# Where the output projection's weights are loaded, and a re-cut order, in a fused attention and MLP kernel

## The chip, the cores and the metric

The kernel runs on one core of a Trainium2 chip. The metric is the device time of one execution in microseconds; the time before is the median of three runs. The profile is of one further execution.

## What is computed

```
xn  = layernorm(x)                                   # 2048 tokens x 640
q   = (xn @ wq) as 32 heads of 20;  k = xn @ wk;  v = xn @ wv   # one k and v for all heads
A   = softmax(q k^T / sqrt(20)) v, heads joined, @ wo
B   = silu(xn @ w1) @ w2                             # 640 -> 1728 -> 640
out = x + A + B
```

All inputs and the output are bf16.

## The kernel before

A scheduler written in Python lays out the whole program before it is built. Each step is an `Op` with an engine, an estimated duration and the steps that it depends on; the scheduler gives every engine a fixed list, in which it runs on the chip, with semaphores where one engine needs another's result.

The work is cut into four chunks of 512 queries (`QC`, `QW`), and each chunk into 8 groups of 4 heads, 32 groups in all. A group has 64 score blocks: 4 heads by 16 tiles of 128 keys. TensorE makes each block (line 1090, one head in one of the four row groups of the array, so that up to four run side by side) into one of 7 PSUM banks of 512 columns. A block is then turned into softmax weights by one of two engines. ScalarE takes one, two or three neighbouring banks at a time by an exponential (line 1114). Or VectorE clamps one block to integers (line 1130); three such make a set, and two shifted copies of it are added up by VectorE (1594) or GpSimd (1600). TensorE multiplies the weights with v in steps of up to four matmuls, one for each head, in four column groups (line 1168), into an eighth bank. At the end of a group VectorE casts that bank to SBUF (`Uev`, line 1644, tensor sbt13), SP issues a DMA transpose of it (line 1613, into sbt14), VectorE takes the reciprocal of the sums (line 1627), and GpSimd scales (1632).

Between these, TensorE works off jobs (line 649): the projection of q for the next chunk, the MLP's two layers and the output projection for the last one. A job is done in whole steps of four column groups, or a step is cut into four quarter pieces that ride in a run of scores (line 1268). VectorE evicts q (line 1745, tensor sbt5), and SP then copies it head by head to its place in sbt9 (line 1754, five to eight DMAs for each).

From the 64th score block on TensorE's list isn't planned but written out by hand: `ORDER` has one letter for each step (a or A a score block for ScalarE, where A closes the exponential; d or D one for VectorE; p a step of PV; j a whole step of a job; k a quarter piece), `BANKS` the bank of each, and `SETS` which blocks each p takes. The other engines' lists follow from it by the scheduler's rules. On SP, DMAs of the names `dma` and `xTd` go in the order in which they were made; the others go when the scheduler finds them ready. An `Op` with a time in `at` isn't placed ahead of that time of the plan (lines 345 to 346); `RES_AT` is 96.0, and the eight residual loads (`load_res`, line 1931) have it.

The tensor qT (sbt9) has two halves, for the chunk in work and for the next. Before q may be copied in, a half is filled from `qo` (sbt19) by one DMA (`qz`, line 2244; 1 MB for the half of chunk 1). `late_loads` is called at the end of group 0 (`norm_dma`, line 1610, when `g == LATE_G`) and makes the loads that can't go sooner, since the first stage uses that memory: 15 loads of w2 (sbt3, line 2033), 5 of wo (sbt6, line 2254) and the fill. After the fill VectorE zeroes a part of `qo` (line 2257).

## Time and profile before

| | |
|---|---|
| runs | 676.49, 677.92, 678.03 us; median 677.92 |
| profiled execution | 676.2 us, of which 674.4 us are the span from first to last instruction |
| PE, ACT busy | 99%, 97% of the span |
| DVE, POOL busy | 93%, 82% |
| DMA, mean busy share of 16 engines | 0.17 |
| exponentials of line 1114 | 680, busy 597.7 us |
| loads of wo | 5 of 160 KB, issued by SP from 60.64 us on |

Line numbers are those of the kernel before. PE is TensorE's matmuls, PEld its weight loads, DVE VectorE, ACT ScalarE, POOL GpSimd, SP the queue that issues nearly all DMAs. Times in the timelines count from the start of the span. A timeline's row is merged from neighbours of one line: start, duration, engine, line, operation, output and input, count, and in brackets the idle time ahead with what ended it.

### The profile page before, as it was taken

The numbers are of one execution on the slowest core, as the hardware profiler recorded it, in microseconds if no ns is written. First come the engines' busy times: TensorE is split into PE (matmuls) and PEld (weight loads), VectorE is DVE, ScalarE is ACT, GpSimd is POOL, SyncE is SP. The second block draws the span as 40 slices with busy tenths as digits, with TensorE's granted clock in tenths as the row PEclk, the third lists the DMA queues.
The fourth block names the chain that finished last, engine by engine and source line by source line (L and its number), as shares of the span: only waits on it lengthen the run. The fifth ranks groups of instructions, "written<-read, shape, count | busy, mean of one in ns | idle before, by whom it ended". The sixth has DMA issues, their size and how long they took to land.

```text
span 674.4 us, 22180 instructions
## 1 busy us (share of the span) xinstructions
PE 666.3 (99%) x9683; PEld 224.6 (33%) x9686; DVE 629.7 (93%) x1130; ACT 653.5 (97%) x790; POOL 556.1 (82%) x440
## 2 busy tenths in 40 slices
PE   9999999999999999999999999999999999999998
PEld 4333233323332333333333333333333333233344
DVE  7998899999999999999999999999999999999994
ACT  6999899999999999999999999999999999999994
POOL 5577798788877898888889889988888889988892
PEclk9999899999999999999999999999999999999999
DMA  7557130001013000020103001101012010000012
GB/s 208 106 187 236 49 93 10 10 18 10 18 23 51 10 11 9 18 37 18 29 18 69 22 10 10 26 16 31 10 29 66 20 29 10 8 4 20 20 27 75
DMA packets 53239, 28.14 MB, mean 42 GB/s; under 512 B 39094, under 2 KB 52502, under 8 KB 53142
## 3 DMA queue, kind: packets, MB, share of 16 engines
q1 hardware_dynamic: 52854, 26.40, 15.5%
q8 instruction: 76, 1.25, 0.7%
q10 hardware_dynamic: 288, 0.33, 0.2%
q14 instruction: 21, 0.17, 0.1%
HBM read 11.44 MB, written 2.62 MB: 21 GB/s over the span
## 4 chain that ended last, share of the span: by engine, by line
PE 93%; DVE 4%; ACT 1%; POOL 1%; DMA 0%; issue 0%; ACTq 0%
PE psall L1168 33%; PE psall L1090 28%; PE psall L649 27%; DVE sbt L1130 2%; PE psall L1353 1%; ACT sbt L1549 1%; POOL sbt L1600 1%; PE psall L1526 1%; PE psall L1441 1%; PE psall L1268 1%; PE psall L2285 1%; PE psall L1775 0%; DMA sbt<-sbt 0%; DVE sbt L1594 0%; DVE sbt L1566 0%
## 5 line engine op out<-in xcount | busy, mean ns | idle before, releaser
L1114 ACT ACTIVATE sbt<-psall 128x1024 bf16<-128x1024 f32 (+1 forms) x680 | 597.7, 1036 | 5.2 <-PE psall L1090 4.6
L1600 POOL TENSOR_TENSOR sbt<-sbt 128x768 int32<-128x768 int32 (+1 forms) x369 | 520.6, 1437 | 91.2 <-DVE sbt L1594 83.0
L1130 DVE TENSOR_SCALAR sbt<-psall 128x512 int16<-128x512 f32 x703 | 452.9, 682 | 24.8 <-PE psall L1090 15.7
L1168 PE MATMUL psall<-sbt 128*32 128x512 bf16 x3410 | 280.4, 385 | 0.0
L1090 PE MATMUL psall<-sbt 32*128 32x512 bf16 x1967 | 251.5, 385 | 1.7 <-DVE sbt L1130 1.3
L649 PE MATMUL psall<-sbt 128*32 128x320 bf16 (+1 forms) x3663 | 228.7, 332 | 0.0
L1090 PEld LDWEIGHTS psall<-sbt 32*128 32x128 bf16 x1967 | 66.7, 91 | 229.4 <-ACT sbt L1114 89.2
L649 PEld LDWEIGHTS psall<-sbt 128*32 128x32 bf16 x3663 | 80.5, 95 | 83.6 <-issue 47.9
L1168 PEld LDWEIGHTS psall<-sbt 128*32 128x32 bf16 x3410 | 68.8, 95 | 100.6 <-issue 76.8
L1594 DVE TENSOR_SCALAR sbt<-sbt 128x1536 int16<-128x1536 int16 (+1 forms) x129 | 72.9, 581 | 0.3
L1268 PE MATMUL psall<-sbt 32*128 32x320 bf16 (+1 forms) x200 | 64.7, 325 | 0.2 <-DVE sbt L1130 0.2
L1794 DVE SCALAR_TENSOR_TENSOR sbt<-sbt,psall 128x512 bf16<-128x512 bf16 (+1 forms) x56 | 37.9, 679 | 0.7 <-ACT sbt L1786 0.4
L1786 ACT ACTIVATE sbt<-psall 128x512 bf16<-128x512 f32 x54 | 38.2, 708 | 0.0
L1549 ACT ACTIVATE sbt<-psall 128x1024 bf16<-128x1024 f32 (+2 forms) x28 | 27.8, 1071 | 0.3 <-PE psall L1526 0.2
L1632 POOL TENSOR_TENSOR sbt<-sbt 128x320 bf16<-128x320 bf16 x31 | 22.5, 727 | 3.5 <-DVE sbt L1594 2.7
L1644 DVE CAST sbt<-psall 128x512 bf16<-128x512 f32 x31 | 21.1, 681 | 0.0
L1268 PEld LDWEIGHTS psall<-sbt 32*128 32x128 bf16 x200 | 18.0, 90 | 5.5 <-issue 2.4
L1892 DVE SCALAR_TENSOR_TENSOR sbt<-psall,sbt 128x320 bf16<-128x320 f32 x28 | 13.3, 486 | 5.4 <-PE psall L649 3.9
L1353 PE MATMUL psall<-sbt 128*128 128x512 bf16 (+4 forms) x57 | 15.7, 422 | 1.4 <-DVE sbt L2048 1.2
L2140 POOL TENSOR_SCALAR sbt<-sbt 128x640 bf16<-128x640 bf16 x9 | 7.8, 874 | 10.6 <-DVE sbt L2144 10.5
L1566 DVE TENSOR_SCALAR sbt<-psall 128x512 int16<-128x512 f32 x22 | 14.8, 686 | 1.0 <-PE psall L1526 0.8
L2114 DVE BATCH_NORM_STATS2 sbt<-sbt 128x6 f32<-128x320 bf16 x26 | 11.4, 472 | 2.5 <-DMA sbt<-in_A_x_dram 2.5
(84 smaller groups left out, 125.6 us busy)
## 6 DMA issues: line engine op xcount, KB each, us to landing
sbt<-in_A_x_dram SPq DMA_DIRECT2D x31, 160.0 KB, 3.0
out_dram<-sbt SPq DMA_DIRECT2D x15, 160.0 KB, 1.8
sbt<-in_B_w_dram SPq DMA_DIRECT2D x5, 432.0 KB, 6.1
sbt<-sbt SPq DMA_DIRECT2D x105, 20.0 KB
sbt<-in_B_w_dram SPq DMA_DIRECT2D x13, 160.0 KB, 3.0
sbt<-sbt SPq DMA_DIRECT2D x1, 1024.0 KB, 5.8
sbt<-sbt SPq DMA_TRANSPOSE x58, 2.5
sbt<-in_A_wo_dram SPq DMA_DIRECT2D x5, 160.0 KB, 3.3
```

What stands on the lines that cost most here:

```text
L649: ins = pe.matmul(self.bk(b, 0, n, j, j + SLOT), w[:, j:j + SLOT], x, start=start, stop=stop, tile_position=(0, j), skip_group_check=True)
L1090: return pe.matmul(self.bk(b), self.kT[row:row + SLOT, kt * P:(kt + 1) * P], self.qT[row:row + SLOT, g % 8, (g // 8) % 2, :], start=True, ...
L1114: return a.activation(self.E[:, b0 * QW:(b0 + n) * QW], self.ps[:, b1 * BANK:(b1 + n) * BANK], AF.Exp, scale=ACT_SCALE, bias=ACT_BIAS)
L1130: return v.tensor_scalar(self.Z[:, zs, zp * QW:(zp + 1) * QW], self.bk(b), 0.0, ZMAX, ALU.max, ALU.min)
L1168: ins = pe.matmul(self.bk(UBANK, 0, QW, r, r + SLOT), self.v[:, it.w, it.kt, :], it.x(), start=f, stop=False, tile_position=(0, r), skip_g ...
L1268: return pe.matmul(self.bk(b, 0, n), w[r0:r0 + SLOT, :], x[r0:r0 + SLOT, :], start=first, stop=last, tile_position=(r0, 0), skip_group_che ...
L1549: return a.activation(self.E[:, (b0 + lo) * QW:(b0 + lo + m) * QW], self.ps[:, b * BANK:(b + m) * BANK], AF.Exp, scale=ACT_SCALE, bias=ACT ...
L1594: sc.new("dve", td, lambda v, k=k: v.tensor_scalar(self.Y[:, zs, k, 0:w], self.Z[:, zs, 0:w], float(PH[k + 1][0]), None, ALU.add), zk, yk, ...
L1600: sc.new("pool", tp, lambda v, k=k, cb=cb: v.tensor_tensor(self.Y[:, zs, k, 0:w].bitcast(I32), self.Z[:, zs, 0:w].bitcast(I32), cb, ALU.ad ...
L1632: op = sc.new(eng, 0.75 if eng == "pool" else t_dve_ps(16 * DH), lambda v: v.tensor_tensor(dst, ut[:, :, :, 0:DH], rb, ALU.mult), [key, (" ...
L1786: sc.new("act", t_act(QW), lambda a: a.activation(t, src, AF.Tanh, scale=0.5), [("B", b)], [("tb", tp)], prio=X_PRIO, name=f"th{c}_{fk}")
L1794: sc.new("dve", t_dve_ps(QW), lambda v, r0=r0, r1=r1, ht=ht: v.scalar_tensor_tensor(out=ht[r0:r1, :], in0=t[r0:r1, :], scalar=1.0, in1=src ...
```

## The change

In `late_loads` the fill is made ahead of wo's loads, and wo's loads get `RES_AT` as their earliest time. The tables `ORDER`, `BANKS` and `SETS` are replaced as a whole; the shares of their letters stay nearly the same (3925 letters become 3915).

```
@@ load_w
                 op.deps = set(deps)
                 op.inc_no = len(pieces)
+                if key == "o":
+                    op.at = RES_AT
             sc.note(op, (), [tag])
@@ late_loads
             load_w2([key])
+            qz(1, [key])
             load_w("sp", "o", [lambda q, c=c: q.dma_start(self.wo[:, c, :], self.A_wo[c * P:(c + 1) * P, :])
                                for c in range(DC)], ("wo",), P * D * 2, (), [key])
-            qz(1, [key])
@@ ORDER
-    "ppaADppdaAaAddppDApaDaApppAAkpjdaAkjjjaAdkppdakAppaAkjpppDDaApjjaADkppDaAkjpaDkAjjjjjdaAppaADppDaAdp"
...
+    "paADpppDaAaAddpppdAApppaDAapDApjjDaAjjaAjppaADpaAkjpjpDaAdjpjaAdkppaAdkpkadApjjjjjadAppaAdppdaAppDa"
...
```

The first place is SP's list from group 0's transposes (the first row, sbt14 from sbt13) to group 1's (the last). The difference of the two programs, with - for before and + for the change; the line numbers behind the edit go up by two or three.

```order
 L1613 DMA_TRANSPOSE sbt14<-sbt13 128x4x128
-L2033 DMA sbt3<-in_B_w2_dram 128x640 x13
-L2033 DMA sbt3<-in_B_w2_dram 64x640 x2
-L2254 DMA sbt6<-in_A_wo_dram 128x640 x5
-L2244 DMA sbt9<-sbt19 128x8x512
+L2035 DMA sbt3<-in_B_w2_dram 128x640 x13
+L2035 DMA sbt3<-in_B_w2_dram 64x640 x2
+L2246 DMA sbt9<-sbt19 128x8x512
 L1754 DMA sbt9<-sbt5 12x512
 L1754 DMA sbt9<-sbt5 20x512 x5
 L1754 DMA sbt9<-sbt5 16x512
 L1613 DMA_TRANSPOSE sbt14<-sbt13 128x4x128
```

The five loads of wo have left; the fill follows w2 directly, and the rest stands as it stood. In the batch of copies behind the last row one copy of 4 rows moves from the sixth place to the first.

The second place is SP's list where wo's loads have gone, from the residual loads (sbt21 and sbt20) to the transposes of group 3.

```order
 L1931 DMA sbt21<-in_A_x_dram 128x640 x4
 L1931 DMA sbt20<-in_A_x_dram 128x640 x4
+L2257 DMA sbt6<-in_A_wo_dram 128x640 x5
 L1613 DMA_TRANSPOSE sbt14<-sbt13 128x4x128
 L1754 DMA sbt9<-sbt5 20x512 x6
```

They stand behind all eight residual loads and ahead of these transposes.

The third place is VectorE's list in the changed program, from the cast of group 1's sums (L1644) over their reciprocal (L1627) to the zeroing of `qo`, which is L2259 here. L1130 evicts scores, L1794 is the MLP's, and L1745 evicts q.

```order
L1644 CAST sbt13<-psall 128x512
L1130 TENSOR_SCALAR sbt11<-psall 128x512 x3
L1794 SCALAR_TENSOR_TENSOR sbt15<-sbt18,psall 128x512
L1130 TENSOR_SCALAR sbt11<-psall 128x512
L1745 TENSOR_SCALAR sbt5<-psall 128x512
L1130 TENSOR_SCALAR sbt11<-psall 128x512
L1627 RECIPROCAL sbt31<-sbt14 128x16
L1130 TENSOR_SCALAR sbt11<-psall 128x512 x7
L2259 MEMSET sbt19 64x256
```

The list of before has the same rows from the cast to the reciprocal; behind it four evictions stood ahead of the zeroing, where seven stand now.

## The prediction

> **What bounds the kernel now.** First the page's first part, for the engines' shares.

> ```profile
> PE 666.3 (99%) x9683; PEld 224.6 (33%) x9686; DVE 629.7 (93%) x1130; ACT 653.5 (97%) x790; POOL 556.1 (82%) x440
> ```

> Two engines are full, TensorE and ScalarE. Which waits for which is asked of the table of waits (engine, line and what it waited for; us in total, times, longest):

> ```profile
> PEld psall L1090 <- ACT sbt L1114: 89.2, 239, 0.6
> ...
> ACT sbt L1114 <- PE psall L1090: 4.6, 4, 2.8
> ...
> DVE sbt L1627 <- DMA sbt<-sbt: 2.1, 2, 1.9
> ```

> Score matmuls (L1090) wait 239 times for an exponential (L1114) to empty a bank; the exponentials wait for scores only 4 times, and one of those waits is 2.8 of the 4.6 us. So ScalarE paces the middle of the kernel, and anything that lets ScalarE run dry is added to the time. The third row is a rare thing beside it: VectorE's reciprocal of a group's sums (L1627) waited for a DMA, once for 1.9 us. To see whether the two belong together I cut the time into windows (busy us and count of PE, PEld, DVE, ACT, POOL; then granted clock, DMA share, GB/s).

> ```profile
> 66.00:68.00 2.00, 2.00 (x36) 0.66 (x24) 2.00 (x5) 2.00 (x3) 2.00 (x3) 1.00 1.08 385
> 68.00:70.00 2.00, 2.00 (x30) 0.62 (x26) 1.98 (x4) 2.00 (x4) 2.00 (x2) 1.00 0.43 138
> 70.00:72.00 2.00, 2.00 (x33) 0.48 (x25) 1.69 (x3) 2.00 (x3) 2.00 (x3) 1.00 0.11 32
> 72.00:74.00 2.00, 1.06 (x14) 0.31 (x10) 0.46 (x2) 2.00 (x5) 1.28 (x2) 1.00 0.33 76
> 74.00:76.00 2.00, 1.60 (x13) 0.55 (x17) 2.00 (x4) 0.58 (x2) 2.00 (x3) 0.58 0.08 21
> 76.00:78.00 2.00, 2.00 (x19) 0.32 (x11) 0.95 (x3) 0.59 (x1) 1.45 (x2) 0.56 0.09 23
> ```
> ```profile
> PEclk9999899999999999999999999999999999999999
> ```

> They do. VectorE is nearly idle from 72 to 74 us, then TensorE, then ScalarE (0.58 and 0.59 of 2 us), and from 74 to 78 us the granted clock is 0.58 and 0.56. The page's slices of the clock, each 16.9 us, show no other dip: the one 8 holds this place.

> VectorE's timeline (start, duration, line; in brackets the idle time before it) shows who was late:

> ```profile
> 60.37 0.68 DVE L1745 TENSOR_SCALAR sbt<-psall 128x512 bf16<-128x512 f32 x1
> ...
> 66.71 0.68 DVE L1644 CAST sbt<-psall 128x512 bf16<-128x512 f32 x1
> ...
> 71.01 0.68 DVE L1130 TENSOR_SCALAR sbt<-psall 128x512 int16<-128x512 f32 x1
> 73.54 0.25 DVE L1627 RECIPROCAL sbt<-sbt 128x16 f32<-128x16 bf16 x1 [1.85 <-DMA sbt<-sbt]
> ```

> Group 1's sums are cast to SBUF at 66.71 to 67.39 us, and the reciprocal that needs them transposed is reached at 71.69. That is 4.3 us, and it was not enough. The SP queue's timeline and a row of the chain of waits tell why.

> ```profile
> 53.06 7.54 SPq L2033 DMA_DIRECT2D sbt<-in_B_w_dram  x15
> 60.64 3.25 SPq L2254 DMA_DIRECT2D sbt<-in_A_wo_dram  x5
> 63.94 0.70 SPq L2244 DMA_DIRECT2D sbt<-sbt  x1
> 64.76 5.81 SPq L1754 DMA_DIRECT2D sbt<-sbt  x7
> 71.02 1.25 SPq L1613 DMA_TRANSPOSE sbt<-sbt  x1
> ...
> 94.65 3.90 SPq L1931 DMA_DIRECT2D sbt<-in_A_x_dram  x8
> 112.78 1.21 SPq L1613 DMA_TRANSPOSE sbt<-sbt  x1
> ```
> ```profile
> 71.02 2.50 DMA sbt<-sbt
> ```

> The transposes (L1613) stand behind 15 loads of w2, 5 of wo, the fill of q's other half (L2244) and 7 copies of q. SP was busy from 53.06 to 70.57 without a gap worth naming, so they went out at 71.02, though their data stood ready at 67.39, and landed 2.50 later, at 73.52.

> **The change, part by part.** *The five loads of wo leave the place ahead of the fill.* Their row is 3.25 us of SP, 3.29 to the start of the fill. The fill then starts at 60.64 and the seven copies at 64.76 - 3.29 = 61.47. The first copy also waits for VectorE's L1745, which ended at 61.05, so that doesn't hold it. Seven copies take 5.81 and end at 67.28; the cast ends at 67.39, so the transposes go out at about 67.5 and land at 70.0. VectorE reaches the reciprocal at 71.69: 1.7 us to spare instead of 1.85 short. The order of VectorE between cast and reciprocal is the same in both programs (third piece of order above), so nothing moves this meeting point but the work ahead. The data in the DMA engines doesn't stand against it: their share was 1.08 at 66 to 68 us and 0.43 after, with wo's 0.8 MB (5 x 128 x 640 x 2 bytes) among it; without it the backlog ends sooner. Behind the transposes SP's next batch of copies now begins with the 4-row copy, which waits for the seven copies; issued by 67.28, they have the transposes' own 2.50 us and more to land, so it holds nothing. What is late next is nothing on VectorE's queue: the steps behind the reciprocal are evictions of scores that were waiting.

> What is the wait worth? TensorE and ScalarE around it:

> ```profile
> 71.41 0.61 PE L1168 MATMUL psall<-sbt 128*32 128x512 bf16 x8
> 71.96 0.39 PE L1090 MATMUL psall<-sbt 32*128 32x512 bf16 x3
> 72.28 0.40 PE L1168 MATMUL psall<-sbt 128*32 128x512 bf16 x4
> 72.61 0.45 PE L1090 MATMUL psall<-sbt 32*128 32x512 bf16 x3
> 74.40 0.60 PE L1090 MATMUL psall<-sbt 32*128 32x512 bf16 x1 [1.33 <-DVE sbt L1130]
> 74.93 1.90 PE L1168 MATMUL psall<-sbt 128*32 128x512 bf16 x16
> 76.76 0.61 PE L1090 MATMUL psall<-sbt 32*128 32x512 bf16 x4
> 77.30 0.59 PE L1168 MATMUL psall<-sbt 128*32 128x512 bf16 x4
> 77.83 0.39 PE L1090 MATMUL psall<-sbt 32*128 32x512 bf16 x3
> ```
> ```profile
> 77.41 2.96 ACT L1114 ACTIVATE sbt<-psall 128x1024 bf16<-128x1024 f32 x4 [2.83 <-PE psall L1090]
> ```

> By ScalarE it is 2.83 us, its idle time. By TensorE: starts at full clock are 0.32 us after a run of scores, 0.33 after one step of four PV matmuls, and 0.22 more for each further step (0.55 for two). From 72.61 stand a run of four scores, four PV steps, a run and one step: 0.33 + 0.99 + 0.32 + 0.33 = 1.97, so 77.83 should have been 74.58, and the loss is 3.25. The engine that sets the pace is ScalarE, so I take **-2.83** and keep -3.25 for the range. The 1.33 us of idle is less than half of either; the rest is the clock.

> [...]

> *The loads of wo come back behind the eight residual loads*, at about 98.6 us (94.65 + 3.90). They take 3.25 there and end at 101.8. The next thing on SP starts at 112.78, so 11 us hide them; were that cover gone, group 3's transposes would be late by up to 3.25. Who reads wo comes much later: it is used for chunk 0's output, and the first store of output (row of line L1901: shortest, median and longest ns, first and last start) is issued at 296.5.

> ```profile
> L1901 SPq DMA_DIRECT2D out_dram<-sbt x15: 332/344/1545, 296.5 to 670.7; - x15
> ```

> The value is 0.

> *The fill and the zeroing of qo.* The fill only moves forward by 3.3 us; the memset that waits for it now stands three evictions later on VectorE. 0.

> *The new order.* Counted from the two tables: runs of scores 611 before, 610 now; score matmuls of the table 1967 and PV matmuls 3410 in both; 200 quarter pieces become 184, which makes 4 more whole steps (3663 matmuls of line L649 become 3679); exponentials over one, two, three banks 98, 580, 2 before and 95, 583, 1 now. The exponentials have rows of their own when shapes are kept apart:

> ```profile
> L1114 ACT ACTIVATE sbt<-psall 128x1024 bf16<-128x1024 f32 x580 | 551.4, 1099 | 3.8 <-PE psall L1090 3.3 <-PE psall L1268 0.2
> ...
> L1114 ACT ACTIVATE sbt<-psall 128x512 bf16<-128x512 f32 x98 | 54.5, 648 | 1.4 <-PE psall L1090 1.3
> ...
> L1114 ACT ACTIVATE sbt<-psall 128x1536 bf16<-128x1536 f32 x2 | 3.1, 1542 | 0.0
> ```

> Busy time over count is 0.556, 0.951 and 1.55 us (the means overlap, so they aren't used). Three of one bank and one of three go, three of two come: 1.67 + 1.55 - 2.85 = **-0.37**. The rest of the order I bound. Above: four whole steps of 0.22 less one run of 0.32 are +0.56, if TensorE had no room; the 89.2 us that it waits for ScalarE say it has. Below: the other three waits of the exponentials, 4.6 - 2.8 = 1.8, could all go. No row says they do, and I take 0, near the first.

> The sum: 2.83 + 0.37 = 3.20. The profiled execution took 676.2 us, 1.8 around its span of 674.4, so by its own measure 673.0. The median of the runs shown, 677.92, lies 1.72 above the profiled one. Neither is more likely to be repeated, so I go half way: **673.9**.

> **The rivals** (same half-way scale).

> *B: one wait of this size remains.* SP is still full until the transposes, or a new meeting point misses. For it: the cast ends 0.1 us from the end of the copies and nothing but the copies' 5.81 us is between them and the fill. Against: 1.7 us to spare. Only the exponentials' 0.37 is left: 676.7.

> *C: the new order makes such waits elsewhere (slower).* VectorE runs in a fixed order, and there are 31 such reciprocals (32 groups, the last apart); where copies of q stand right ahead of the transposes, as here,

> ```profile
> 167.31 6.29 SPq L1754 DMA_DIRECT2D sbt<-sbt  x8
> 173.65 1.21 SPq L1613 DMA_TRANSPOSE sbt<-sbt  x1
> ```

> a reciprocal moved 2 us forward would wait. It decides from where the transposes land over 1.3 us after VectorE gets there, since that much idle was enough to lose the clock; each costs 2.83, or 3.25 by TensorE. One gives B's time; two give 679.5, or 680.4 by TensorE's price, three 682.4. Against: in the trace of before 29 of 31 don't wait.

> *D: the dip of the clock is not the wait's.* Then only 1.33 + 0.37 is won: 675.4. Against: the dip begins with the idle gap, and no other slice has one.

> **How the numbers follow.** Forecast A 0.75, B 0.12, C 0.07, D 0.06. This kernel's measurement tells about 0.3% from no change, here 2 us: faster means under 675.9. A gives 0.73 of faster and D 0.05, so 0.78; B, and the edges of A, C and D, 0.17 of same; C 0.05 of slower. Low end: the forecast less 0.4 (TensorE's 3.25) and less 1.8 of the exponentials' waits, 671.7. High end: B's 676.7 and a little, 676.9; C is left out.

> **What would show it.** Right: the reciprocal of group 1 without idle before it, transposes issued near 67.5, clock 1.00 from 60 to 80 us, ScalarE 19.9 of 20 there, 679 exponentials by L1114, and wo's loads near 98.6. From 80 us on every step should stand about 3 us earlier and stay so to the end. Wrong: a bracket of over 1 us before any L1627, a second stretch with a clock near 0.5, or a lead at 80 us that is gone by 640.

## The result, and the profile after

The changed kernel takes 673.08 us (median of six runs, 672.76 to 673.87), the kernel before 677.85 (six runs, 675.67 to 679.45): a ratio of 0.9936, with a 95% interval of 0.9917 to 0.9955. The profiled execution took 673.7 us with a span of 671.9, against 676.2 and 674.4: 2.5 less, where the medians are 4.8 apart.

The page of the changed kernel, its engines and its clock:

```profile
PE 663.3 (99%) x9683; PEld 224.5 (33%) x9686; DVE 629.6 (94%) x1130; ACT 653.3 (97%) x789; POOL 556.5 (83%) x440
...
PEclk9999999999999999999999999999999999999999
```

TensorE does the same 9683 matmuls in 3.0 us less busy time (666.3 before), and the one 8 of the clock is gone. The table of waits of the changed kernel (us in total, times, longest):

```profile
PEld psall L1090 <- ACT sbt L1114: 93.0, 248, 0.8
...
ACT sbt L1114 <- PE psall L1090: 2.0, 4, 0.9
...
DVE sbt L1627 <- DMA sbt<-sbt: 1.5, 3, 0.7
```

The exponentials still wait for scores four times, but the longest wait is 0.9 us where it was 2.8. ScalarE paces the middle as before; TensorE waits for it a little more. The place of the old stall, from VectorE's timeline of the changed kernel (start, duration, in brackets the idle time ahead):

```profile
66.36 0.68 DVE L1644 CAST sbt<-psall 128x512 bf16<-128x512 f32 x1
...
70.66 0.68 DVE L1130 TENSOR_SCALAR sbt<-psall 128x512 int16<-128x512 f32 x1
72.05 0.26 DVE L1627 RECIPROCAL sbt<-sbt 128x16 f32<-128x16 bf16 x1 [0.70 <-DMA sbt<-sbt]
```

The wait for the transposes is 0.70 us instead of 1.85. It is not gone. The windows of the changed kernel around it (busy us and count of PE, PEld, DVE, ACT, POOL; then clock, DMA share, GB/s):

```profile
70.00:72.00 2.00, 2.00 (x30) 0.51 (x31) 1.34 (x3) 2.00 (x3) 2.00 (x2) 1.00 0.27 4
72.00:74.00 2.00, 1.97 (x23) 0.45 (x21) 1.95 (x5) 2.00 (x3) 2.00 (x3) 1.00 0.09 23
74.00:76.00 2.00, 2.00 (x27) 0.58 (x25) 2.00 (x5) 1.74 (x4) 2.00 (x2) 1.00 0.09 25
76.00:78.00 2.00, 2.00 (x32) 0.55 (x28) 2.00 (x5) 2.00 (x3) 0.50 (x2) 1.00 0.09 23
```

VectorE's gap no longer reaches the others: TensorE idles 0.03 us, ScalarE 0.26, and the clock stays at 1.00. SP's timeline of the changed kernel shows the new places:

```profile
53.15 7.54 SPq L2035 DMA_DIRECT2D sbt<-in_B_w_dram  x15
60.73 0.70 SPq L2246 DMA_DIRECT2D sbt<-sbt  x1
61.55 6.53 SPq L1754 DMA_DIRECT2D sbt<-sbt  x7
68.13 1.25 SPq L1613 DMA_TRANSPOSE sbt<-sbt  x1
70.84 19.53 SPq L1754 DMA_DIRECT2D sbt<-sbt  x13
...
91.68 3.90 SPq L1931 DMA_DIRECT2D sbt<-in_A_x_dram  x8
95.62 2.33 SPq L2257 DMA_DIRECT2D sbt<-in_A_wo_dram  x5
109.77 1.21 SPq L1613 DMA_TRANSPOSE sbt<-sbt  x1
```

The fill follows w2, the copies follow the fill, and the transposes go out at 68.13 instead of 71.02. wo's loads stand at 95.62 and end 11.8 us ahead of the next thing on SP. The transposes landed 3.9 us after their issue, not 2.50; the trace of DMAs, for the window 68.1 to 72.2 us of the changed kernel (queue, packets, MB, share; then the issue and us to landing), has something beside them:

```profile
q8 instruction: 1, 0.02, 2.1%
...
sbt<-sbt SPq DMA_TRANSPOSE x1, 3.9
```

That is one packet of instructions (queue q8). What it has to do with the landing is asked below.

### The profile page after: what moved, and what is told of

The parts are those of the page before. It is cut to its first block, busy times and chain, and to the rows that moved or that the text cites. A ratio compares the mean times of both kernels' runs of the same rounds, so it can differ in the third digit from the quotient of the medians.

```text
span 671.9 us, 22178 instructions
## 1 busy us (share of the span) xinstructions
PE 663.3 (99%) x9683; PEld 224.5 (33%) x9686; DVE 629.6 (94%) x1130; ACT 653.3 (97%) x789; POOL 556.5 (83%) x440
## 3 DMA queue, kind: packets, MB, share of 16 engines
q8 instruction: 76, 1.25, 0.8%
## 4 chain that ended last, share of the span: by engine, by line
PE 68%; ACT 28%; DVE 3%; DMA 1%; issue 0%; ACTq 0%; DVEq 0%
ACT sbt L1114 25%; PE psall L1168 24%; PE psall L649 20%; PE psall L1090 20%; ACT sbt L1549 2%; ACT sbt L1786 1%; DVE sbt L2116 1%; PE psall L1526 1%; PE psall L1268 1%; DMA sbt<-sbt 1%; PE psall L1441 1%; DVE sbt L1130 0%; DMA sbt<-in_A_x_dram 0%; PE psall L1775 0%; PE psall L2287 0%; DVE sbt L1566 0%
## 5 line engine op out<-in xcount | busy, mean ns | idle before, releaser
L1114 ACT ACTIVATE sbt<-psall 128x1024 bf16<-128x1024 f32 (+1 forms) x679 | 596.8, 1028 | 2.4 <-PE psall L1090 2.0
L1130 DVE TENSOR_SCALAR sbt<-psall 128x512 int16<-128x512 f32 x703 | 453.4, 683 | 22.4 <-PE psall L1090 14.8
L1168 PE MATMUL psall<-sbt 128*32 128x512 bf16 x3410 | 279.9, 383 | 0.4 <-DVE sbt L1644 0.2
L1090 PE MATMUL psall<-sbt 32*128 32x512 bf16 x1967 | 250.1, 384 | 0.7 <-ACT sbt L1114 0.5
L649 PE MATMUL psall<-sbt 128*32 128x320 bf16 (+1 forms) x3679 | 230.4, 332 | 0.0
L1090 PEld LDWEIGHTS psall<-sbt 32*128 32x128 bf16 x1967 | 66.5, 90 | 225.1 <-ACT sbt L1114 93.0
L649 PEld LDWEIGHTS psall<-sbt 128*32 128x32 bf16 x3679 | 81.0, 95 | 83.4 <-issue 48.1
L1168 PEld LDWEIGHTS psall<-sbt 128*32 128x32 bf16 x3410 | 68.9, 94 | 100.0 <-issue 74.1
L1594 DVE TENSOR_SCALAR sbt<-sbt 128x1536 int16<-128x1536 int16 (+2 forms) x129 | 71.8, 572 | 0.3
L1268 PE MATMUL psall<-sbt 32*128 32x320 bf16 (+1 forms) x184 | 59.2, 324 | 0.0
L1794 DVE SCALAR_TENSOR_TENSOR sbt<-sbt,psall 128x512 bf16<-128x512 bf16 (+1 forms) x56 | 38.0, 680 | 0.9 <-ACT sbt L1786 0.9
L1644 DVE CAST sbt<-psall 128x512 bf16<-128x512 f32 x31 | 21.2, 682 | 0.1
L1268 PEld LDWEIGHTS psall<-sbt 32*128 32x128 bf16 x184 | 16.6, 90 | 6.9 <-issue 3.5
```

The lines of the kernel that those rows point to most:

```text
L649: ins = pe.matmul(self.bk(b, 0, n, j, j + SLOT), w[:, j:j + SLOT], x, start=start, stop=stop, tile_position=(0, j), skip_group_check=True)
L1090: return pe.matmul(self.bk(b), self.kT[row:row + SLOT, kt * P:(kt + 1) * P], self.qT[row:row + SLOT, g % 8, (g // 8) % 2, :], start=True, ...
L1114: return a.activation(self.E[:, b0 * QW:(b0 + n) * QW], self.ps[:, b1 * BANK:(b1 + n) * BANK], AF.Exp, scale=ACT_SCALE, bias=ACT_BIAS)
L1130: return v.tensor_scalar(self.Z[:, zs, zp * QW:(zp + 1) * QW], self.bk(b), 0.0, ZMAX, ALU.max, ALU.min)
L1168: ins = pe.matmul(self.bk(UBANK, 0, QW, r, r + SLOT), self.v[:, it.w, it.kt, :], it.x(), start=f, stop=False, tile_position=(0, r), skip_g ...
L1268: return pe.matmul(self.bk(b, 0, n), w[r0:r0 + SLOT, :], x[r0:r0 + SLOT, :], start=first, stop=last, tile_position=(r0, 0), skip_group_che ...
```

## The experiments

Three theories stood at first. The theory of the **queue** (the prediction's): wo's 3.3 us on SP hold the transposes back, the late reciprocal lets TensorE and ScalarE run dry, and the clock falls for that. Its rival, the theory of the **tables**: the new `ORDER`, `BANKS` and `SETS` bring the gain, wherever wo stands. A second rival, the theory of the **fill**: what matters is that the fill's 1 MB moves sooner and wo's 0.8 MB isn't in the DMA engines beside it, not the place on SP's list. Two more came up on the way: which stretch of a stall makes the clock fall, and why the transposes land late in the changed kernel.

Every ratio below is against runs of the kernel before on the same chip, whose medians were 676.98, 677.36 and 677.36 us in the three sets (e1 to e4, e5 to e8, e9 to e11).

### e1: the move alone, with the old tables

The edit, to the kernel before:

```
@@ load_w
+                if key == "o":
+                    op.at = RES_AT
@@ late_loads
             load_w2([key])
+            qz(1, [key])
             load_w("sp", "o", [lambda q, c=c: q.dma_start(self.wo[:, c, :], self.A_wo[c * P:(c + 1) * P, :])
...
-            qz(1, [key])
```

> The tables of before; only the loads of wo are moved (fill first, wo behind the residual loads). Theory 1, the meeting of group 1's transposes and VectorE: the reciprocal waits 0 to 0.7 us instead of 1.85, TensorE has no idle gap of over 1 us near 73, no half clock, and 2.8 to 3.3 us less than before: about 674.7. Theory 2, the new order of the tables brings the gain: no more than 0.5 us less than before, about 677.5.

Measured: 674.03 us (673.5 to 674.43), ratio 0.9952 (0.9937 to 0.9967). The span is 672.1, the clock has no dip, and the reciprocal waits 0.30. VectorE's timeline of e1:

```profile
66.61 0.69 DVE L1644 CAST sbt<-psall 128x512 bf16<-128x512 f32 x1
71.90 0.25 DVE L1627 RECIPROCAL sbt<-sbt 128x16 f32<-128x16 bf16 x1 [0.30 <-DMA sbt<-sbt]
88.86 0.68 DVE L1644 CAST sbt<-psall 128x512 bf16<-128x512 f32 x1
```

From group 1's cast to group 2's are 22.25 us; before they were 25.12 (66.71 to 91.83). The move alone takes the stall away.

### e2: the new tables alone, wo where it was

The edit, to the changed kernel:

```
@@ load_w
-                if key == "o":
-                    op.at = RES_AT
@@ late_loads
             load_w2([key])
-            qz(1, [key])
             load_w("sp", "o", [lambda q, c=c: q.dma_start(self.wo[:, c, :], self.A_wo[c * P:(c + 1) * P, :])
...
+            qz(1, [key])
```

> The tables of the change; the loads stand as before (wo ahead of the fill). Theory 1: the transposes of group 1 go out at about 71, the reciprocal waits 1.5 to 2 us, the clock falls to half behind it, and only 0.4 us is won: about 677.4. Theory 2: about 673.5, and a wait at the reciprocal costs nothing.

Measured: 675.05 us (674.13 to 678.43), ratio 0.9976 (0.9963 to 0.9989). The stall is back, and VectorE's and TensorE's timelines of e2 show it whole:

```profile
73.87 0.25 DVE L1627 RECIPROCAL sbt<-sbt 128x16 f32<-128x16 bf16 x1 [1.90 <-DMA sbt<-sbt]
```
```profile
75.32 0.39 PE L1090 MATMUL psall<-sbt 32*128 32x512 bf16 x2 [1.54 <-DVE sbt L1130]
```

So the tables don't remove it: the theory of the tables fell as the cause of the stall's end. But they gave 1.9 us of median with the stall in place, more than the 0.37 that I had counted, and more than the 0.4 that was expected here (677.4); about 0.6 of it is that fewer of e2's runs have a dip of the clock (see the spread of the runs below). And the clock stayed at 1.00 behind a gap of 1.54 us, longer than the 1.33 that came before the dip.

### e3: the fill first, but wo still ahead of the copies

The edit, to the kernel before:

```
@@ late_loads
             load_w2([key])
+            qz(1, [key])
             load_w("sp", "o", [lambda q, c=c: q.dma_start(self.wo[:, c, :], self.A_wo[c * P:(c + 1) * P, :])
...
-            qz(1, [key])
```

> The tables of before; the fill goes ahead of wo's loads, but wo's loads stay ahead of the seven copies and the transposes. Theory 1, SP's issue time is what counts: the same five issues stand ahead of the transposes, they go out at about 71, and the time is that of before, 677.8, within 0.5. Theory 3, the fill's 1 MB should be out of the way sooner, its place in the data stream is what counts: the transposes land earlier, and 1 us or more is won.

Measured: 678.96 us (677.26 to 679.89), ratio 1.0024 (1.0012 to 1.0035). SP's timeline of e3:

```profile
61.17 0.70 SPq L2244 DMA_DIRECT2D sbt<-sbt  x1
61.91 4.66 SPq L2255 DMA_DIRECT2D sbt<-in_A_wo_dram  x5
66.69 5.23 SPq L1754 DMA_DIRECT2D sbt<-sbt  x7
72.37 1.25 SPq L1613 DMA_TRANSPOSE sbt<-sbt  x1
```

The fill goes out early, and the transposes later than ever (72.37), since five loads behind a 1 MB fill take SP 4.66 us instead of 3.25. The reciprocal waits 2.69, TensorE 2.17, and the clock is at half for two windows. The fill's own place brings nothing, so that half of its theory fell, and what counts is what SP issues ahead of the transposes. The other half, wo's data in the DMA engines, e3 leaves as it was; against it stands that the transposes landed 2.4 to 2.5 us after their issue both with wo ahead (before, e2, e3) and without it (e4, e6). The time itself was expected to stay within 0.5 of before, and is 2.0 longer.

### e4 and e6: w2's loads moved too

The edit, to the changed kernel:

```
@@ load_w
                 if key == "o":
                     op.at = RES_AT
+                elif key == "2":
+                    op.at = 76.0
@@ late_loads
-            load_w2([key])
             qz(1, [key])
+            load_w2([key])
...
-            np_("dve", 0.3, lambda v: v.memset(self.qo[0:FLAST, :], 0.0), [], [("qo",)], prio=2.0, name="zero")
+            np_("dve", 0.3, lambda v: v.memset(self.qo[0:FLAST, :], 0.0), [], [("qo",)], prio=2.0, name="zero").at = 73.0
```

> The change, and also the 15 loads of w2 go behind the next batch of copies of q (the memset of qo is pinned so that every other engine's order stays that of the change). Group 1's transposes then have 7.5 us less of SP ahead of them. Theory 1: they go out when the cast ends, about 67.1, land by 69.6, and the 0.70 us that the reciprocal still waits in the change is gone; 0.4 to 0.7 us less than the change: about 672.5. Theory 4, the landing is late by the load of instructions that falls on it and not by the queue: the wait stays at about 0.7 and the time is that of the change, 673.1.

Measured: 672.5 us (671.86 to 673.09), ratio 0.9932 (0.9915 to 0.9949), span 670.1. SP's timeline of e4:

```profile
52.90 0.70 SPq L2248 DMA_DIRECT2D sbt<-sbt  x1
60.47 5.16 SPq L1754 DMA_DIRECT2D sbt<-sbt  x7
66.81 1.22 SPq L1613 DMA_TRANSPOSE sbt<-sbt  x1
70.55 5.89 SPq L1754 DMA_DIRECT2D sbt<-sbt  x8
76.48 8.80 SPq L2037 DMA_DIRECT2D sbt<-in_B_w_dram  x15
```

SP now stands idle until q is ready, the transposes go out as soon as the cast ends (66.09 + 0.68 = 66.77), and the reciprocal has no wait. w2's loads are issued in 76.48 to 85.28. Beside the change on one chip:

> e4 once more beside the change. Theory 1: no wait at the reciprocal, 0.4 to 0.7 us less than e5. Rival: e4's gain came from another chip or another job, and e5 and e6 agree within 0.2 us.

Measured: 672.79 us (672.46 to 673.22), ratio 0.9933 (0.9913 to 0.9954), 0.84 below the change in the same set (e5). The ranges of the two overlap, but five of e5's six runs lie above all of e6's.

### e5: the change once more

> The change once more, on the same chip as e6 to e8. By the same theory as its first profile: a wait of 0 to 0.7 us at group 1's reciprocal, no half clock, about 673.1, and a spread of its runs of about 1 us, since there is no idle gap of TensorE for the clock to fall on.

Measured: 673.63 us (672.38 to 673.66), ratio 0.9942 (0.9919 to 0.9964). Transposes at 68.16, the wait 0.73, no dip: as in the first profile (68.13 and 0.70).

### e7: the kernel before once more

> The kernel before once more, for its stall. Theory 5, the clock is judged in fixed windows of 3.41 us that lie anywhere against the program: the reciprocal waits 1.6 to 2.2 us and TensorE idles 1.2 to 1.6 us as in the first profile; if most of that idle lies in one window, the half clock follows and the profiled run is near 677; if it is split over two as in e2, there is none and the run is near 675.5. Rival: the idle gap's length alone decides, then the half clock comes here as it did in the first profile.

Measured: 676.86 us (675.33 to 679.44), ratio 1.0001; the profiled execution took 676.84. Transposes at 71.70, the wait 2.31 and TensorE's gap 1.80, all longer than in the first profile, and the clock does not fall. The prediction's reading of the clock, by the length of a gap, did not hold. Theory 5 as it was put here missed too: 1.35 of the gap's 1.80 us lie in one window of 3.41, and no half clock follows.

### e8: three of wo's loads stay ahead

The edit, to the kernel before, with the fill ahead of wo as in e1:

```
@@ load_w
-            for f in pieces:
+            for i, f in enumerate(pieces):
...
+                if key == "o" and i >= 3:
+                    op.at = RES_AT
```

> The tables of before, the fill first; three of the five loads of wo stay behind it, ahead of the copies and the transposes, two go behind the residual loads. Theory 1: the transposes go out about 1 us sooner than before, at about 70, the reciprocal waits 0.8 to 1.2 us, TensorE idles under 0.8 us, and the half clock no longer comes: between e1 and before, about 675.3. Rival, all or nothing: the gain needs all five loads moved, and the time is that of before.

Measured: 675.27 us (674.59 to 676.18), ratio 0.9968 (0.9954 to 0.9981). The transposes went out at 71.42, not 1 us sooner than before: the fill took SP 1.55 us instead of 0.70, and the three loads behind it 3.02. The wait was 1.84, TensorE's gap 1.33, the same as in the first profile of the kernel before, and again there is no dip. The expected step of the issue time was missed. But this profile is the slowest of e8's twelve runs (676.18), and the median is the 675.3 that was expected, so the stall was probably shorter in the others; they left no trace, so that is not shown. For the clock the two profiles are the cleanest pair, with one gap and two outcomes.

### e9: the change with two loads staying ahead

The edit, to the changed kernel:

```
@@ load_w
-            for f in pieces:
+            for i, f in enumerate(pieces):
...
-                if key == "o":
+                if key == "o" and i >= 2:
```

> The change, but two of wo's five loads stay behind the fill, ahead of the copies and the transposes. The transposes of group 1 then go out 1 to 1.5 us later than in the change, at about 69.5 to 70. Theory 6, in the change the transposes landed late (3.9 us from issue to landing) because a load of instructions ran on the DMA engines from 69.15 to 70.51: here their packets start after it, land 2.4 us after the issue, and the reciprocal waits 0.6 to 1.0 us, hardly more than in the change; the time is that of the change plus 0 to 0.4 us. Rival: the long landing belongs to this place whatever runs beside it; then they land at 73.5 to 74 and the reciprocal waits over 1.8 us, as before.

Measured: 673.82 us (ten runs, 673.62 to 676.25; the three above 675.4 have a mean granted clock of 0.997, the others 0.998 to 1.000), ratio 0.9957 (0.9941 to 0.9973). The trace of DMAs, window 70 to 73 us of e9, and VectorE's timeline:

```profile
q1 hardware_dynamic: 606, 0.17, 24.1%
...
sbt<-sbt SPq DMA_TRANSPOSE x1, 2.4
```
```profile
72.25 0.25 DVE L1627 RECIPROCAL sbt<-sbt 128x16 f32<-128x16 bf16 x1 [1.16 <-DMA sbt<-sbt]
```

There is no instruction packet in the window, and the transposes land 2.4 us after an issue 1.65 us later than the change's (69.78 against 68.13). The reciprocal runs only 0.20 later than the change's; its wait of 1.16 is a little over the 0.6 to 1.0 expected, since VectorE came to it sooner.

### e10 and e11: two more profiles of the kernel before

> A further look at the stall of the kernel before: the reciprocal waits 1.8 to 2.4 us. Theory 5b: whether the half clock follows depends on how few matmuls start in a window of 3.41 us; under about half of the usual 45 brings it (21 and 18 did, 28 and 29 did not). With the half clock the exponentials lose 1.3 us more than the wait less 0.2; without it just the wait less 0.2.

> As e10: a sample of the same stall, with the same two outcomes.

Measured: 677.01 and 675.99 us. Their waits are 2.23 and 2.86, their gaps of TensorE 1.72 and 2.35. The shorter gap has a half clock behind it, the longer has none. e11's wait is outside the range expected; by starts both fit theory 5b (21 in e10's window, 25 and 28 in e11's).

### The runs together

Times of the profiled executions in us. "Cast to cast" is from group 1's cast (L1644) to group 2's. "By the sum" is explained below.

| | tables | transposes issued | reciprocal waits | TensorE idle | half-clock windows | cast to cast | by the sum | span |
|---|---|---|---|---|---|---|---|---|
| before | old | 71.02 | 1.85 | 1.33 | 1 | 25.12 | 25.1 | 674.4 |
| e7 | old | 71.70 | 2.31 | 1.80 | 0 | 24.26 | 24.3 | 675.0 |
| e10 | old | 71.36 | 2.23 | 1.72 | 1 | 25.46 | 25.5 | 675.2 |
| e11 | old | 71.96 | 2.86 | 2.35 | 0 | 24.81 | 24.8 | 674.1 |
| e8 | old | 71.42 | 1.84 | 1.33 | 0 | 23.78 | 23.8 | 674.4 |
| e3 | old | 72.37 | 2.69 | 2.17 | 2 | 27.22 | 27.2 | 678.0 |
| e1 | old | 68.63 | 0.30 | 0 | 0 | 22.25 | 22.3 | 672.1 |
| e2 | new | 71.43 | 1.90 | 1.54 | 0 | 23.66 | 23.7 | 672.6 |
| after | new | 68.13 | 0.70 | 0 | 0 | 22.47 | 22.5 | 671.9 |
| e5 | new | 68.16 | 0.73 | 0 | 0 | 22.49 | 22.5 | 671.7 |
| e9 | new | 69.78 | 1.16 | 0.49 | 0 | 22.92 | 22.9 | 671.8 |
| e4 | new | 66.81 | 0 | 0 | 0 | 21.93 | 21.9 | 670.1 |
| e6 | new | 67.50 | 0 | 0 | 0 | 21.92 | 21.9 | 671.0 |

**What the stall costs.** All rows follow one sum: 22.15 us with the old tables or 21.95 with the new, plus the reciprocal's wait less 0.2 (where it is longer than that), plus 1.3 for each window at half clock. The constants are fitted to these thirteen rows, which it meets within 0.05. So nearly all of the wait goes on to the end, even the 0.7 that leaves TensorE busy, and one half-clock window costs 1.3.

**The spread of the runs.** The timed runs left no trace, but the mean granted clock of each is on record. In the profiles one window of 3.41 us at half clock takes 0.0025 off that mean, and a slow tail at the end up to 0.0015 more (e3), so 0.998 and up is read as no dip, 0.996 and 0.997 as one window, 0.993 to 0.995 as two. Of the 75 runs of the kernel before in the three sets and in e7, e10 and e11, 24 have none (median 676.13 us), 40 one (677.38) and 11 two (679.05). So the dips make some 3 of the 4.7 us that these runs spread over, 1.25 for the first and 1.67 for the second, where the sum gives 1.3 each. All twelve runs of the change (its first six and e5) are at 0.999 or 1.000. The same reading parts e2's gain: without a dip e2 and the kernel before have medians of 674.80 and 676.16 in their set (seven runs each), 1.36 apart; with one, 675.95 and 677.24, 1.29 apart.

**What makes the clock fall.** In the traces half clock comes in stretches of 3.41 us (74.33 to 77.74 before) or twice that (75.17 to 82.00 in e3), and it begins a whole number of 3.41 us steps behind the start of full clock: before, full clock lasts from 6.06 to 74.33, which is 68.27 us or 20.0 steps. In the changed kernel full clock starts at 4.20, so the grid lies at another place of the program there. The stall can be cut along that grid. That the clock is judged step by step on it, as e7's theory has it, is an estimate of mine from these times. Windows of the kernel before, the one ahead of the dip and the dip (PEld's count is the weight loads in the window, one for each matmul):

```profile
70.92:74.33 3.41, 2.14 (x29) 0.57 (x21) 1.56 (x5) 3.41 (x6) 2.69 (x3) 1.00 0.22 52
74.33:77.74 3.41, 3.34 (x25) 0.77 (x25) 2.36 (x6) 0.58 (x2) 3.12 (x3) 0.50 0.10 25
```

The same two of e10, which dips:

```profile
72.79:76.20 3.41, 1.69 (x24) 0.53 (x21) 2.39 (x5) 1.67 (x4) 2.30 (x3) 1.00 0.19 44
76.20:79.61 3.41, 3.41 (x30) 0.76 (x30) 2.33 (x6) 2.27 (x4) 1.51 (x2) 0.50 0.08 20
```

And of e3, which dips for two windows:

```profile
71.76:75.17 3.41, 1.75 (x21) 0.47 (x18) 0.72 (x3) 3.27 (x6) 1.85 (x3) 1.00 0.23 55
75.17:78.58 3.41, 2.90 (x21) 0.66 (x21) 2.45 (x5) 0.00 (x0) 3.41 (x3) 0.50 0.11 27
78.58:82.00 3.42, 3.42 (x30) 0.75 (x30) 2.13 (x4) 2.38 (x4) 0.15 (x1) 0.50 0.03 8
```

Against them e11 and then e7, cut along their own grids, with no dip:

```profile
70.55:73.97 3.42, 2.41 (x29) 0.59 (x25) 1.04 (x2) 3.42 (x7) 2.50 (x2) 1.00 0.24 58
73.97:77.38 3.41, 2.07 (x28) 0.73 (x28) 2.92 (x7) 0.85 (x3) 2.59 (x3) 1.00 0.10 24
```
```profile
73.77:77.18 3.41, 2.06 (x28) 0.73 (x28) 2.91 (x7) 1.40 (x4) 2.58 (x3) 1.00 0.10 24
```

And e8, whose gap is as long as before's:

```profile
73.44:76.85 3.41, 2.11 (x28) 0.77 (x28) 2.97 (x7) 1.88 (x5) 2.70 (x4) 1.00 0.08 21
```

In these stalls, windows with 18 or 21 starts are followed by half clock, windows with 25 or 28 are not; a full window has about 45 (45 in 67.50 to 70.91 before). e3's second window, with 21 starts, keeps half clock for the third. Busy time sorts them less well (2.14 us in before's, which dips, and 2.06 in e7's, which doesn't). The clock fell behind gaps of 1.33, 1.72 and 2.17 us and not behind 1.33, 1.54, 1.80 and 2.35, so their length doesn't sort them. Where the gap falls on the grid does: e11's 2.35 us are spread over two windows, before's 1.33 fall into one that was thin already, and e8's 1.33 into one that was not. The pages of before and after count 9683 matmuls to 9686 weight loads, those of e1 and e3 9686 to 9686, so single records can be missing. The bound is known only as between 21 and 25, and it is a fit to seven stalls.

Starts alone don't sort all windows. In the first 30 us of these traces windows with 15 to 20 starts keep the full clock, as this one of e3 and the window behind it:

```profile
20.56:23.97 3.41, 2.37 (x15) 1.02 (x15) 3.15 (x16) 3.41 (x4) 1.07 (x2) 1.00 0.48 109
23.97:27.38 3.41, 3.17 (x43) 1.79 (x43) 3.34 (x9) 3.29 (x5) 1.73 (x2) 1.00 0.58 131
```

Most matmuls there have the form 128*128, rows by columns of the array (15 of 15, 10 of 19 and 13 of 19 in the changed kernel's windows from 4.20, 14.44 and 21.27 us), those of the stall 32*128 or 128*32. Weigh each matmul by its share of the array and by its columns out of 512: the windows ahead of a fall then have 4.5 to 5.25 (21 starts of a quarter each), and every other window of the thirteen traces has 5.62 or more, until TensorE runs out of work at the end. That sorts some 2500 windows, but it too is a fit to what happened, and no run varied it on purpose.

**Why the transposes land late.** In the changed kernel the instruction packet of 16 KB ran from 69.15 to 70.51 us, across the packets of the transposes (69.36 to 71.35); alone these take 0.6 to 0.7 (72.25 to 72.97 before). With such a packet across them they landed after 3.9 (after), 4.3 (e5) and 3.2 us (e1). In the ten other traces, where it ends ahead of them (before, for one) or begins behind them (e4, e6), they landed after 2.4 to 2.5. The packets show the pause itself: in the changed kernel 473 of the transposes' 512 end by 69.98, none from there to 70.54, and the last 39 (an even share of one engine of sixteen would be 32) behind the end of the instruction packet at 70.51; in e5 the pause lasts to 70.98, its instruction packet to 70.95. e9 was made to tell this: sent 1.65 us later they missed the packet and landed in 2.4. That the packet holds them up fits all thirteen traces and the pause in their packets; a kernel without the packet was not tried, so the cause is supported and not shown.

## Why the prediction was right

The forecast was 673.9, the median 673.08, and e5's 673.63. The mechanism, wo's loads ahead of the transposes on SP, is the one predicted. That the number came so near is partly luck: the stall's price was put some 0.4 too high and the order's gain some 0.9 too low. By its steps:

*The stall and its owner.* Right. Move wo away and the stall goes (e1); leave it and the stall stays, with any tables (e2, e3). Rival B, a remaining wait of that size, is out. So is C: of the 31 reciprocals of the changed kernel three wait for a DMA, 1.5 us in all, and the longest of these waits is the 0.7 of group 1.

*"Transposes go out at about 67.5 and land at 70.0 ... 1.7 us to spare."* Wrong, and by more than it looks: 68.13, 72.0, and 0.70 short. Of the 2.4 us between the two, the landing made 1.4 (3.9 instead of 2.50), the issue 0.6, as the copies took SP 6.53 us instead of 5.81, and VectorE came to the reciprocal 0.35 sooner. I took both durations over from a place with different traffic beside it. The wait that remains costs 0.5 by the sum, which e4 and e6 won back. "Without a gap worth naming" left out 0.45 us besides, from the last copy to the transposes (70.57 to 71.02): they are there in all six traces with all five loads of wo ahead and shrink to 0.04 to 0.06 in the change, e1, e5, e8 and e9, for a cause not found.

*The stall's price, -2.83.* About right as a size: cast to cast fell from 25.12 to 22.47, that is 2.65, of which 0.2 belongs to the tables. But its make-up was not as told. The prediction had TensorE's idle as "less than half" and "the rest is the clock". By the sum 1.65 was the wait, 1.3 the clock, and 0.5 is still there. And the clock's part is not in every execution: of four profiles of the kernel before two have the dip, and by the mean clock 51 of its 75 runs.

*"Over 1.3 us idle was enough to lose the clock."* Wrong as a rule: 1.33 did it once and did not in e8, and neither 1.80 (e7) nor 2.35 (e11) did. I had one stall to read it from. Rival D, that the dip is not the wait's, the runs refute as well: half clock comes in three of the seven traces in which TensorE idles 1.33 us or more, and in none of the six with 0.49 or less. Its forecast of 675.4 is missed, since the wait's own price is greater than TensorE's idle.

*wo's loads cost nothing behind the residual loads.* Right: 95.62 (predicted near 98.6, since all stands 3 us earlier), 2.33 us on SP instead of 3.25, and SP free until 109.77.

*The new order, -0.37.* Too small, and the term that was mis-sized most. The counts were right: the exponentials by form in the changed kernel are

```profile
L1114 ACT ACTIVATE sbt<-psall 128x1024 bf16<-128x1024 f32 x583 | 553.0, 1092 | 0.3
...
L1114 ACT ACTIVATE sbt<-psall 128x512 bf16<-128x512 f32 x95 | 52.6, 633 | 2.1 <-PE psall L1090 2.0
```

But take from each span what its stall cost (cast to cast less 22.15 or 21.95): the seven kernels with the old tables then have 671.4 to 672.9, mean 672.2, and the six with the new 670.1 to 671.4, mean 670.9. The order is worth about -1.3, give or take 0.6 from their spread, and e2's runs against those of before with as many dips (-1.36 and -1.29) agree. By the same traces 0.2 of it comes between the casts of groups 1 and 2, and 0.54 from there to group 30's cast, where no trace of one order reaches into the range of the other (554.6 to 554.9 us with the old tables, 554.1 to 554.4 with the new). The rest, 0.4 ahead of group 1's cast and 0.15 at the end, is within the spread. Which waits the new order saves was not settled; the term's bound of -1.8 held it.

The sum in the trace: about -2.45 for the stall (25.12 - 22.15 less the 0.5 that remains) and about -1.3 for the order make -3.7, predicted -3.20. The two first profiles show only -2.5 because of their ends: at group 2's cast the change leads by 3.00 us and at group 30's by 3.29, as forecast, and 0.8 are lost behind that, where the kernel before took 28.0 us and the change 28.8; the thirteen traces take 28.0 to 29.0 there, with either tables. The medians show -4.8 and, in e5, -3.7.

*The signs.* Besides the wait and the transposes, ScalarE was busy 19.74 of the 20 us from 60 to 80 (19.9 expected), the clock there is 1.00, and the exponentials are 679.

What stays open: which waits the new order saves, why the wait of the kernel before differs from run to run (1.85 to 2.86 us in four profiles), and what exactly makes the clock fall. The medians of the first comparison are 1.1 further apart than the sum; by the number of dips a median of the kernel before can stand 1.3 higher or lower, but the clocks of those six runs are not on record.

## What to carry to other kernels

Read an issuing queue like an engine: SP was busy without a gap for 17.5 us, and a small transfer on which three engines depended stood behind loads whose first result is stored at 296.5 us. The fix is to move what isn't urgent, and e4 and e6 show that it pays to go on until the urgent transfer goes out the moment its data is ready. Don't take a margin on such a queue from durations at another place: issue and landing both came out longer at the new one, and a predicted 1.7 us to spare became 0.7 short. And take several profiles before pricing a clock dip: it came in two of four profiles of one kernel, and by the mean clock in 51 of 75 runs.
